# Two-bank PSUM reads for gelu, gate product, mask, exponential and remainder, with a new step list

## The chip, the cores and the metric

The kernel runs on one core of one Trainium2 chip. The time is the device time of one launch in microseconds. Three runs of the kernel before gave 258.43, 259.08 and 259.88 us; the median is 259.08 us.

## The reference, cut to what matters

A gated linear recurrence over 768 tokens feeds a GEGLU block with a gated residual.

```python
# attention: batch 4, heads 8, tokens 768, head size 48
scale = np.minimum(mag, 0.999) / (mag + 1e-06)        # mag = |a|
new_re = ar * S_re - ai * S_im                         # complex decay, per key row
new_im = ar * S_im + ai * S_re
S_re, S_im = (new_re + kv, new_im)                     # kv = k v^T
y[:, :, t] = np.einsum('bhd,bhde->bhe', q[:, :, t], S_re)
# feed-forward on x: [3072, 384], d_ff 1536
g, val = x @ w_gate, x @ w_val
ffn_out = (0.5 * g * (1 + erf(g / sqrt(2))) * val) @ w_out
out = x + ffn_out / (1 + exp(-(x @ w_res)))
```

## The kernel before, in words

The 768 tokens are cut into 6 chunks of 128. A *tile* is one batch and one chunk: 24 tiles of 128 tokens x 384 values. Tiles are grouped into 14 *units*; `SIZES` gives units of one tile (numbers 0, 1, 12, 13) and ten of two tiles. Each unit goes through three functions, which only record steps:

- `prepare`: loads a_re, a_im, q, k and v. ScalarE takes logarithms and exponentials (`ln`, `exp`, `lnb`), and arctangents. The decay's logarithm and its angle are each split into two 16-bit parts (`lh`, `ll`; `th`, `tl`) and summed over the tokens on TensorE with a triangular matrix (`cumL`, `cumT`, one PSUM bank for each tile). ScalarE evicts the first sums twice, as exp and exp of the negative (`pexpE`, `pexpI`, L427 and L428); from the second sums it takes the number of turns (`round`, L461), and VectorE the remainder of the angle (`fr`, L463). Sines, cosines and magnitudes make the features of q and k (`feat`), which are transposed on TensorE or by DMA.
- `attend`: per tile, eight heads of K^T Q in two banks of four heads (`qk`, L535); VectorE masks each bank (`am`, L538); `av` multiplies by v and adds the state's part; `kv` makes the state's update, which VectorE adds to the old state (`U`), and which is scaled by the decay into a bf16 copy (`Gb`) and an fp32 copy (`Gf`).
- `forward`: x is transposed; for each of six pairs of d_ff blocks, six matmuls fill a gate bank and six a value bank (`gv`, L606). ScalarE takes the gelu of the gate bank into an SBUF buffer (`gelu`, L611), VectorE multiplies it by the value bank (`h`, L612). `res` and `tanh` make the residual gate, `out` (L632) multiplies by w_out, `ot` and `otx` finish, and SP stores.

The steps are numbered as they are recorded: 1,442 of them. `ORDER` is a list of those numbers, written out by hand, and the instructions are issued in that order. Each engine so has a fixed sequence, and waits at its next instruction until what it needs is there. `PLACE` gives the engine for steps that VectorE, ScalarE or GpSimd could do. `Plan.run` also hands out buffers: at its first use each PSUM bank, tag `pb`, 8 of them, goes to the least recently ended one. Steps of VectorE and GpSimd that use a shared port (`TWO_PORTS`, and GpSimd's own work) are chained: where the list turns from one of the two engines to the other, the later step waits for the earlier. A new ScalarE function table is loaded where the list goes from one group of functions (log and exp; arctan and sine; gelu and tanh) to another: 33 times.

SP's queue issues the 120 loads, 28 transposes of features, 20 of x and 24 stores, also in list order; GpSimd's queue issues the weights and the small moves between chunks (`mrd`, `carry`).

Of the kernel before, what the change touches and what calls it, by code (L numbers as in the profile page):

```python
# [9 lines left out]
FP = mybir.dt.float32  # L10
# [8 lines left out]
SIZES = [(1, 1, 2)] + [(2, 2)] * 4 + [(2, 1, 1)]  # L19
PE_X = 3  # L20
PE_T = 6
WD = 21
WH = 8
TWO_PORTS = {"tai", "sq", "la", "lh", "ll", "abs", "th", "tl", "mrc", "qe", "feat", "vcast", "Gb", "Gf", "otx"}
# [5 lines left out]
    23: "POOL", 24: "POOL", 33: "DVE", 44: "POOL", 53: "ACT", 64: "ACT", 105: "DVE", 114: "ACT", 117: "POOL", 121: "DVE",  # L30
    145: "ACT", 190: "DVE", 191: "DVE", 203: "ACT", 213: "DVE", 223: "DVE", 227: "DVE", 228: "DVE", 230: "ACT", 252: "ACT",
    291: "DVE", 305: "DVE", 306: "DVE", 333: "POOL", 345: "ACT", 347: "ACT", 353: "DVE", 357: "DVE", 363: "DVE", 366: "POOL",
    408: "DVE", 422: "DVE", 423: "DVE", 438: "POOL", 446: "DVE", 456: "DVE", 460: "DVE", 469: "DVE", 472: "POOL", 482: "POOL",
    518: "DVE", 539: "DVE", 551: "ACT", 554: "ACT", 562: "DVE", 565: "POOL", 566: "POOL", 572: "DVE", 576: "DVE", 577: "DVE",
    579: "ACT", 588: "POOL", 595: "DVE", 598: "POOL", 670: "ACT", 671: "POOL", 681: "POOL", 682: "POOL", 689: "ACT",
    691: "ACT", 700: "POOL", 710: "POOL", 711: "DVE", 752: "DVE", 767: "POOL", 783: "POOL", 794: "POOL", 801: "ACT",
    803: "ACT", 812: "POOL", 822: "POOL", 823: "DVE", 858: "DVE", 894: "ACT", 902: "DVE", 905: "POOL", 913: "ACT", 924: "POOL",
    991: "POOL", 1003: "ACT", 1006: "POOL", 1017: "POOL", 1025: "ACT", 1042: "DVE", 1045: "POOL", 1080: "DVE", 1086: "DVE",
    1101: "POOL", 1113: "ACT", 1116: "POOL", 1117: "POOL", 1135: "ACT", 1137: "ACT", 1146: "POOL", 1190: "DVE", 1196: "DVE",
    1210: "DVE", 1224: "ACT", 1225: "POOL", 1235: "POOL", 1236: "POOL", 1255: "DVE", 1296: "DVE", 1325: "POOL", 1330: "DVE",  # L40
    1368: "DVE", 1388: "ACT", 1389: "POOL", 1393: "DVE", 1396: "POOL",
}
ORDER = [
# [66 lines left out]
class Store:  # L110


    def __init__(self, tag, bufs):
        self.tag, self.bufs, self.users, self.tile, self.index = tag, bufs, [], None, None
# [15 lines left out]
class Plan:  # L130
# [7 lines left out]
    def store(self, tag, bufs):  # L138
        return Store(tag, bufs)
# [50 lines left out]
def kernel(  # L190
# [13 lines left out]
    nc = tc.nc  # L204
# [476 lines left out]
```

## Time and profile before

The profiled execution took 259.86 us; its span, from the first to the last instruction, is 258.1 us, so 1.76 us lie around it. It is 0.78 us above the median.

| Engine | busy us | share of the span | instructions |
|---|---|---|---|
| TensorE (PE) | 219.4 | 85% | 2362 |
| VectorE (DVE) | 214.4 | 83% | 373 |
| ScalarE (ACT) | 210.4 | 82% | 358 |
| GpSimd (POOL) | 109.7 | 42% | 129 |

The granted clock of TensorE was full throughout. Busy time is the union of an engine's instructions. Two instructions that follow each other overlap by some tens of ns, so means times counts come out above it. A matmul's duration holds its pipeline, so a busy TensorE is not one that issues without a gap.

### The profile page before, as it was taken

What the parts mean: (1) busy time and instruction counts of PE and PEld (TensorE: products, weight loads), DVE (VectorE), ACT (ScalarE), POOL (GpSimd) and SP (SyncE); (2) the same over time, 40 slices, a digit from 0 to 9 for tenths busy, and PEclk for the clock granted to TensorE, in tenths of its full rate; (3) what the DMA queues carried; (4) which work ended last, traced back from release to release, by engine and by line L of the source; (5) the groups of instructions that cost most, each with busy time, mean ns of one, the idle gap of its engine ahead of it and who ended that gap; (6) DMA issues with size and microseconds to landing.
All of it is one profiled execution on the core that took longest, in us unless ns stands there. A gap on an engine that the chain in (4) does not pass through costs nothing.

```text
span 258.1 us, 6191 instructions
## 1 busy us (share of the span) xinstructions
PE 219.4 (85%) x2362; PEld 171.2 (66%) x2362; DVE 214.4 (83%) x373; ACT 210.4 (82%) x358; POOL 109.7 (42%) x129
## 2 busy tenths in 40 slices
PE   0132864769999999999789999999999999999993
PEld 0001453548877887787677767787887868887882
DVE  2499888997999999998988989889998967866363
ACT  5899869989999999999969989999999498331440
POOL 1424145437452395948816386716105514210011
PEclk9999999999999999999999999999999999999999
DMA  8999999997799999789998999799999967862221
GB/s 145 187 194 190 191 184 188 205 221 119 86 164 176 186 171 207 151 152 191 135 219 159 219 173 203 156 168 184 240 155 183 184 141 161 114 113 64 63 91 62
DMA packets 170621, 41.92 MB, mean 162 GB/s; under 512 B 164064, under 2 KB 170592, under 8 KB 170592
## 3 DMA queue, kind: packets, MB, share of 16 engines
q1 hardware_dynamic: 166144, 37.63, 84.0%
q0 software_dynamic: 4448, 3.90, 10.1%
q8 instruction: 18, 0.29, 0.5%
q14 instruction: 11, 0.09, 0.1%
HBM read 31.26 MB, written 4.72 MB: 139 GB/s over the span
## 4 chain that ended last, share of the span: by engine, by line
PE 59%; DVE 11%; DMA 9%; issue 7%; POOL 6%; SPq 4%; ACT 2%; DVEq 0%; POOLq 0%
PE pb L606 29%; PE pb L632 15%; PE pb L621 4%; SPq L383 4%; PE pb L369 3%; DVE h L612 3%; PE pb L535 3%; DMA q<-in_q_dram 2%; POOL t L407 2%; DMA mr<-E 2%; DMA KT<-fK 2%; DMA ai<-in_a_im_dram 2%; DMA t<-fr 2%; PE pb L547 1%; PE pb L504 1%
## 5 line engine op out<-in xcount | busy, mean ns | idle before, releaser
L611 ACT ACTIVATE h<-pb 128x512 bf16<-128x512 f32 (+1 forms) x84 | 41.3, 545 | 21.4 <-PE pb L606 21.0
L606 PE MATMUL pb<-xT,wg 128*128 128x256 bf16 (+1 forms) x504 | 57.0, 257 | 1.3 <-ACT sg L623 0.9
L606 PE MATMUL pb<-xT,wv 128*128 128x256 bf16 (+1 forms) x504 | 56.8, 257 | 0.6 <-DMA xT<-x 0.6
L612 DVE SCALAR_TENSOR_TENSOR h<-h,pb 128x512 bf16<-128x512 bf16 (+1 forms) x84 | 48.5, 603 | 10.4 <-ACT h L611 5.8
L632 PE MATMUL pb<-wo,h 128*128 128x384 bf16 x288 | 53.5, 326 | 0.0
L606 PEld LDWEIGHTS <-wg 128*128 128x128 bf16 x504 | 43.4, 98 | 8.0 <-issue 1.6
L606 PEld LDWEIGHTS <-wv 128*128 128x128 bf16 x504 | 43.3, 98 | 7.2 <-DMA xT<-x 0.8
L648 ACT ACT_TABLE_LOAD x33 | 42.3, 1283 | 1.3 <-PEq L665 0.7
L632 PEld LDWEIGHTS <-h 128*128 128x128 bf16 x288 | 26.5, 97 | 14.3 <-DVE h L612 0.2
L538 DVE TENSOR_TENSOR am<-pb,mask 128x512 bf16<-128x512 f32 x48 | 32.1, 681 | 3.4 <-PE pb L535 3.3
L639 POOL TENSOR_TENSOR ot<-ot,x 128x384 f32<-128x384 f32 x13 | 11.8, 913 | 46.7 <-DVE ot L636 21.7
L369 PEld LDWEIGHTS <-mask 128*128 128x128 bf16 x96 | 9.2, 106 | 27.4 <-issue 24.0
L535 PE MATMUL pb<-QT,KT 96*128 96x128 bf16 x192 | 18.5, 226 | 2.9 <-DMA KT<-fK 1.5
L636 DVE SCALAR_TENSOR_TENSOR ot<-sg,pb 128x384 f32<-128x384 f32 x24 | 13.0, 548 | 7.3 <-PE pb L632 3.3
L407 POOL TENSOR_TENSOR t<-t,ai 128x768 f32<-128x768 f32 (+1 forms) x9 | 13.8, 1542 | 11.0 <-DVE s L412 5.4
L535 PEld LDWEIGHTS <-KT 96*128 96x128 bf16 x192 | 14.1, 101 | 6.7 <-DMA KT<-fK 1.8
L369 PE MATMUL pb<-th,mask 128*128 128x384 f16 x24 | 9.0, 374 | 10.3 <-DVE th L344 10.3
L568 POOL TENSOR_TENSOR Gb<-U,M 96x384 bf16<-96x384 f32 x12 | 9.9, 823 | 15.6 <-DVE fQ L487 7.0
L621 PE MATMUL pb<-wr,xT 128*128 128x384 bf16 x72 | 15.6, 326 | 0.8 <-ACT xT L343 0.8
L573 POOL TENSOR_TENSOR Gf<-U,M 96x384 f32<-96x384 f32 x9 | 7.5, 828 | 19.4 <-DVE tl L455 7.1
L463 DVE SCALAR_TENSOR_TENSOR fr<-fr,pb 128x384 f32<-128x384 int32 x24 | 12.8, 545 | 2.2 <-ACT fr L461 2.2
L369 PE MATMUL pb<-lh,mask 128*128 128x384 f16 x24 | 9.1, 380 | 5.7 <-DVE lh L417 5.7
(89 smaller groups left out, 464.2 us busy)
## 6 DMA issues: line engine op xcount, KB each, us to landing
ar<-in_a_re_dram SPq DMA_DIRECT2D x24, 192.0 KB, 4.7
ai<-in_a_im_dram SPq DMA_DIRECT2D x24, 192.0 KB, 4.5
k<-in_k_dram SPq DMA_DIRECT2D x24, 192.0 KB, 4.3
q<-in_q_dram SPq DMA_DIRECT2D x24, 192.0 KB, 4.2
vf<-in_v_dram SPq DMA_DIRECT2D x24, 192.0 KB, 4.1
out_dram<-ot SPq DMA_DIRECT2D x24, 192.0 KB, 2.6
wg<-in_moe_w_gate_dram POOLq DMA_DIRECT2D x6, 192.0 KB, 6.0
wv<-in_moe_w_val_dram POOLq DMA_DIRECT2D x6, 192.0 KB, 4.3
```

Source lines behind the costliest of these rows:

```text
L369: nc.tensor.matmul(out=bank.tile, lhsT=mask[:, 0, :], rhs=x[:, i * DM:(i + 1) * DM], start=(j == 0), stop=(j == 1))
L407: add(e1, "tai", lambda: on[e1].tensor_tensor(out=F("t"), in0=F("t"), in1=flat(T("ai"), n), op=OP.mult), [s["ai"]], [s["t"]], n)
L463: add("DVE", "fr", lambda i=i: nc.vector.scalar_tensor_tensor(out=T("fr")[:, i], in0=T("fr")[:, i].bitcast(INT), scalar=-TWO_PI, in1=cth[i ...
L535: nc.tensor.matmul(out=ap.tile[:, h, :], lhsT=kT.tile[0:DD, u * H // 2 + h, :], rhs=qT.tile[0:DD, u * H // 2 + h, :], start=True, stop=True)
L538: add("DVE", "am", lambda u=u, am=am, ap=ap: nc.vector.tensor_tensor(out=am.tile[:, u * H // 2:(u + 1) * H // 2, :], in0=ap.tile, in1=mask ...
L606: nc.tensor.matmul(out=o_.tile[:, u, :], lhsT=w_[:, k_, (2 * m + u) * 128:(2 * m + u + 1) * 128], rhs=s["xT"].tile[:, k_, 0:n].rearrange(" ...
L611: add("ACT", "gelu", lambda gp=gp, hv=hv: nc.scalar.activation(out=hv(), in_=gp.tile, func=AF.Gelu), [gp], [hh], n, "G")
L612: add("DVE", "h", lambda vp=vp, hv=hv: nc.vector.scalar_tensor_tensor(out=hv(), in0=hv(), scalar=0.5, in1=vp.tile, op0=OP.mult, op1=OP.mul ...
L621: nc.tensor.matmul(out=rp.tile, lhsT=s["xT"].tile[:, k_, i, :], rhs=wr[:, k_, :], start=(k_ == 0), stop=(k_ == KF - 1))
L632: nc.tensor.matmul(out=op_.tile, lhsT=s["h2"].tile[:, k_, i * 128:(i + 1) * 128], rhs=wo[:, k_, :], start=(k_ == 0), stop=(k_ == NF - 1))
L636: add("DVE", "ot", lambda i=i, op_=op_, ot=ot: nc.vector.scalar_tensor_tensor(out=ot.tile, in0=sg[i].tile, scalar=1.0, in1=op_.tile, op0=O ...
L648: plan.run(ORDER, lambda table: nc.scalar.preload_act_table_set(ACT_SETS[table]), lambda ins, prev: tc.add_manual_dep(ins.ins, prev.ins.na ...
```

## The change: what it does, and the diff

PSUM becomes four fixed tiles of two banks. `Bank(width)` takes one bank or an aligned pair; a single bank is taken preferably beside one that is in use, so that pairs stay whole. What reads PSUM then covers two banks with one instruction:

- `gelu` and `h` of two-tile units: 128x1024 in place of 128x512, three of each for a unit in place of six. One-tile units put four d_ff blocks in one bank, so 128x512 in place of 128x256, again three in place of six. Their twelve matmuls are one step (`gw`).
- the mask of a tile: one 128x1024 instruction (`am2`) in place of two.
- `pexpE`, `pexpI`, `round` and `fr` of two-tile units: one 128x768 instruction in place of two of 128x384.

The gelu's results lie in six small buffers `hb` in place of two large `h2`. The state tiles of two batches share a buffer, and `U` and `Gf` work in place, so `Gf` now comes after `Gb`. A mask `tri` is made on GpSimd at the start and, with `WHOLE = 0`, used by nothing. The options `UG2` and `TN2` are off, so the state's update and tanh stay single. `ORDER` and `PLACE` are new; there are 1,270 steps and 32 table loads.

```diff
+GV2 = 1
+NB1 = 4
+AM2 = 1
+PX2 = 1
+RD2 = 1
 PLACE = { ... }   # new throughout
 ORDER = [ ... ]   # new throughout
...
-                x.index = min(range(x.bufs), key=lambda i: row[i])
-                assert row[x.index] < at[t]
-                row[x.index] = end
+                now = at[t]
+                if x.tag in wide and x.width == 1:
+                    x.index = min(range(x.bufs), key=lambda i: (row[i] >= now, row[i ^ 1] < now, row[i]))
+                else:
+                    x.index = min(range(0, x.bufs, x.width), key=lambda i: max(row[i:i + x.width]))
+                for i in range(x.index, x.index + x.width):
+                    assert row[i] < at[t]
+                    row[i] = end
...
+    banks = [psb.tile([128, 2, 512], FP, tag="ps%d" % i, name="ps%d" % i) for i in range(4)]
     class Bank(Val):
-        def __init__(self):
-            Val.__init__(self, plan.store("pb", 8))
+        def __init__(self, width=1):
+            Val.__init__(self, plan.store("pb", 8, width))
...
+        def tokens(kind, x, hi, lo):
+            if n == 2 and kind[1]:
+                pair = Bank(2)
+                bank = [(pair.part(), lambda i=i: pair.at(i, DM)) for i in range(n)]
...
+            if n == 2 and kind[1]:
+                return [([o for o, _ in bank], slice(0, 2), lambda: pair.both[:, :, 0:DM], 2)]
...
+            if AM2:
+                add("DVE", "am2", lambda am=am, pair=pair: nc.vector.tensor_tensor(
+                    out=am.tile, in0=pair.both.rearrange("p c (h t) -> p (c h) t", t=128),
+                    in1=mask.to_broadcast([128, H, 128]), op=OP.mult), aps, amh)
...
-                    src = Buf("U")
-                        out=src.tile[0:DD], in0=dk.tile[0:DD], in1=old.tile[0:DD], op=OP.add), [dk, old], [src])
+                add("DVE", "U", lambda dkv=dkv, v2=v2: nc.vector.tensor_tensor(out=v2(), in0=dkv(), in1=v2(), op=OP.add), dks, wr_, m)
...
+        nb = 4 // n if n > 1 else NB1
+        w2 = 2 if GV2 and n > 1 else 1
+        for m in range(NF // (nb * w2)):
+            for name, w_ in (("wg", wg), ("wv", wv)):
+                o_ = Bank(w2)
+                for y in range(w2):
...
+            add("ACT", "gelu", lambda gp=gp, hv=hv: nc.scalar.activation(out=hv(), in_=pv(gp), func=AF.Gelu), gs, [hh], sz, "G")
             add("DVE", "h", lambda vp=vp, hv=hv: nc.vector.scalar_tensor_tensor(
-                out=hv(), in0=hv(), scalar=0.5, in1=vp.tile, op0=OP.mult, op1=OP.mult), [vp], [hh], n)
+                out=hv(), in0=hv(), scalar=0.5, in1=pv(vp), op0=OP.mult, op1=OP.mult), vs, [hh], sz)
```

More of the change, by code (lines that the diff above doesn't have):

```diff
@@ L23 @@
 WH = 8
[L24 removed]
+TWO_PORTS = {"tai", "sq", "la", "cap", "lh", "ll", "abs", "th", "tl", "mrc", "qe", "feat", "vcast", "Gb", "Gf", "otx"}
 ISSUES = {"wgv", "wr", "wo", "mrd", "carry"}
@@ L29 @@
 PLACE = {
[L30 to L38, printed above, removed]
@@ L163, in run @@
         at, rows, given, table, last = {}, {}, set(), None, None
+        wide = {x.tag for t in self.steps for x in t.stores if x.width > 1}
         assert sorted(order) == list(range(len(self.steps)))
@@ L220 @@
     size = [len(u) for u in units]
+    groups, at = [], 0
+    for g in FWD:
+        groups.append(list(range(at, at + g)))
+        at += g
+    MT = max(sum(size[p] for p in g) for g in groups)
     ctx.enter_context(tc.manual_schedule())
@@ L229 @@
     mask = cst.tile([128, 1, 128], BF, name="mask")
+    tri = cst.tile([128, 128], FP, name="tri")
     one = cst.tile([128, 1], FP, name="one")
@@ L309, in tile, with part, at, both @@
             return self.store.tile
+    banks = [psb.tile([128, 2, 512], FP, tag="ps%d" % i, name="ps%d" % i) for i in range(4)]
     class Bank(Val):
-        def __init__(self):
-            Val.__init__(self, plan.store("pb", 8))
-        def make(self, shape, dt=FP):
-            self.store.tile = psb.tile(shape, dt, tag="pb%d" % self.store.index, name="pb")
-            return self.store.tile
+        def __init__(self, width=1):
+            Val.__init__(self, plan.store("pb", 8, width))
+        def part(self):
+            return Val(self.store)
+        def at(self, i, *shape, dt=FP):
+            j = self.store.index + i
+            x = banks[j // 2][:, j % 2]
+            if dt != FP:
+                x = x.bitcast(dt)
+            n = 1
+            for y in shape:
+                n *= y
+            x = x[:, 0:n]
+            return x if len(shape) == 1 else x.rearrange("p (a b) -> p a b", b=shape[1])
         @property
-        def tile(self):
-            return self.store.tile
+        def both(self):
+            return banks[self.store.index // 2]
     class Feat(Val):
@@ L362, with whole @@
     st = [dict() for _ in range(NU)]
-    Gf, Gb = [None] * B, [None] * B
+    Gf, Gb, Gs = [None] * B, [None] * B, {}
     def sums(bank, i, hi, lo):
-        bank.make([128, DM])
         for j, x in enumerate((hi, lo)):
-            nc.tensor.matmul(out=bank.tile, lhsT=mask[:, 0, :], rhs=x[:, i * DM:(i + 1) * DM], start=(j == 0), stop=(j == 1))
+            nc.tensor.matmul(out=bank, lhsT=mask[:, 0, :], rhs=x[:, i * DM:(i + 1) * DM], start=(j == 0), stop=(j == 1))
+    def whole(bank, i, x):
+        nc.tensor.matmul(out=bank, lhsT=tri, rhs=x[:, i * DM:(i + 1) * DM], start=True, stop=True)
     def flat(t, n):
@@ new lines, in tokens @@
+        def tokens(kind, x, hi, lo):
+            if n == 2 and kind[1]:
+                pair = Bank(2)
+                bank = [(pair.part(), lambda i=i: pair.at(i, DM)) for i in range(n)]
+            else:
+                bank = [(o, lambda o=o: o.at(0, DM)) for o in (Bank() for _ in range(n))]
+            for i in range(n):
+                if p < WHOLE:
+                    add("PE", "sum" + kind[0], lambda i=i: whole(bank[i][1](), i, F(x)), [s[x]], [bank[i][0]])
+                else:
+                    add("PE", "cum" + kind[0], lambda i=i: sums(bank[i][1](), i, F(hi), F(lo)), [s[hi], s[lo]], [bank[i][0]])
+            if n == 2 and kind[1]:
+                return [([o for o, _ in bank], slice(0, 2), lambda: pair.both[:, :, 0:DM], 2)]
+            return [([bank[i][0]], i, bank[i][1], 1) for i in range(n)]
@@ L429, in prepare @@
+        E, Ei = [], []
+        for src, i, view, m in tokens(("L", PX2), "la", "lh", "ll"):
+            E.append(s["E"].part())
+            Ei.append(s["Ei"].part())
+            act("pexpE", lambda i=i, view=view: nc.scalar.activation(out=T("E")[:, i], in_=view(), func=AF.Exp), src, [E[-1]], "L", m)
+            act("pexpI", lambda i=i, view=view: nc.scalar.activation(out=T("Ei")[:, i], in_=view(), func=AF.Exp, scale=-1.0), src, [Ei[-1]], "L", m)
         s["E"].writers = [x for v_ in E for x in v_.writers]
@@ L519, in f @@
             def f():
-                mp.make([DD, 2 * H])
-                nc.tensor.matmul(out=mp.tile[:, 0:n * H], lhsT=s["mr"].tile[0:n * H].rearrange("x u d -> x (u d)"),
+                nc.tensor.matmul(out=mp.at(0, n * H)[0:DD], lhsT=s["mr"].tile[0:n * H].rearrange("x u d -> x (u d)"),
                                  rhs=idf[0:n * H, 0:n * H], start=True, stop=True)
@@ L578, in forward, with f, state @@
-    def forward(p):
-        s, n = st[p], size[p]
-        s["xT"], s["h2"] = Buf("xT"), Buf("h2")
-        xT = [s["xT"].part() for _ in range(n)]
-        for i in range(n):
+            add(e5, "x", lambda i=i, yp=yp, e5=e5: copy(e5, s["x"].tile[:, i], yp.at(0, H, D)), [yp], [s["xi"][i]])
+        if units[p][0][1] == NC - 1:
+            return
+        c = units[p][0][1]
+        for js in ([list(range(n))] if UG2 else [[i] for i in range(n)]):
+            m, b = len(js), units[p][js[0]][0]
+            dk = Bank(m)
+            dks = [dk.part() for _ in js]
+            for y, i in enumerate(js):
+                def f(i=i, y=y, dk=dk):
+                    for h in range(H):
+                        nc.tensor.matmul(out=dk.at(y, H, D)[:, h, :], lhsT=s["K"].tile[:, i * H + h], rhs=s["v"].tile[:, i, h, :], start=True, stop=True)
+                add("PE", "kv", f, [s["K"], s["v"]], [dks[y]])
+            if m == 2:
+                cut = lambda t: t[0:DD]
+                dkv = lambda dk=dk: dk.both[0:DD, :, 0:DM].rearrange("p c (h d) -> p c h d", d=D)
+                mb = lambda: s["M"].tile[:, 0:2].rearrange("p c (h u) -> p c h u", u=1).to_broadcast([DD, 2, H, D])
+            else:
+                cut = lambda t, b=b: t[0:DD, b % 2]
+                dkv = lambda dk=dk: dk.at(0, H, D)[0:DD]
+                mb = lambda i=js[0]: s["M"].tile[:, i].rearrange("p (h u) -> p h u", u=1).to_broadcast([DD, H, D])
+            def state(tag):
+                key = (tag, b - b % 2, c)
+                if key not in Gs:
+                    Gs[key] = Buf("%s%d" % (tag, b - b % 2))
+                v_ = Gs[key].part()
+                return v_, (lambda cut=cut, g=Gs[key]: cut(g.tile))
+            nb, nbv = state("Gb")
+            olds = sorted({id(Gf[b + y]): Gf[b + y] for y in range(m)}.values(), key=id) if c else []
+            if c > 0:
+                fv = Gf[b].view
+                v2 = (lambda cut=cut, fv=fv: cut(fv()))
+                wr_ = olds
+                add("DVE", "U", lambda dkv=dkv, v2=v2: nc.vector.tensor_tensor(out=v2(), in0=dkv(), in1=v2(), op=OP.add), dks, wr_, m)
+                src, sv = wr_, v2
+            else:
+                src, sv = dks, dkv
+            e14 = place("DVE") if c else "DVE"
+            add(e14, "Gb" if c else "Gb0", lambda nbv=nbv, sv=sv, mb=mb, e14=e14: on[e14].tensor_tensor(
+                out=nbv(), in0=sv(), in1=mb(), op=OP.mult), src + [s["M"]], [nb], m)
+            for y in range(m):
+                Gb[b + y] = nb
+            if c < NC - 2:
+                if c == 0:
+                    nf, nfv = state("Gf")
+                    nf.view = lambda g=Gs["Gf", b - b % 2, c]: g.tile
+                    add("DVE", "Gf0", lambda nfv=nfv, sv=sv, mb=mb: nc.vector.tensor_tensor(
+                        out=nfv(), in0=sv(), in1=mb(), op=OP.mult), src + [s["M"]], [nf], m)
+                    for y in range(m):
+                        Gf[b + y] = nf
+                else:
+                    e6 = place("POOL")
+                    add(e6, "Gf", lambda sv=sv, mb=mb, e6=e6: on[e6].tensor_tensor(
+                        out=sv(), in0=sv(), in1=mb(), op=OP.mult), [s["M"]], src, m)
@@ L583, in forward @@
+    def forward(group):
+        tiles = [(p, i) for p in group for i in range(size[p])]
+        n = len(tiles)
+        xt = Buf("xT")
+        xT = [xt.part() for _ in tiles]
+        for j, (p, i) in enumerate(tiles):
+            s = st[p]
+            flat_x = lambda s=s, i=i: s["x"].tile[:, i].rearrange("p h d -> p (h d)")
             if p >= PE_X:
-                add("SP", "dX", lambda i=i: nc.sync.dma_start(
-                    out=s["xT"].tile[:, :, i, :], in_=s["x"].tile[:, i].rearrange("p h d -> p (h d)"), transpose=True), [s["xi"][i]], [xT[i]])
+                add("SP", "dX", lambda j=j, fx=flat_x: nc.sync.dma_start(out=xt.tile[:, :, j, :], in_=fx(), transpose=True), [s["xi"][i]], [xT[j]])
@@ L614, in forward @@
-        sg = [Buf("sg") for _ in range(n)]
-        for i in range(n):
-            rp = Bank()
-            def f(i=i, rp=rp):
-                rp.make([128, DM])
-                for k_ in range(KF):
-                    nc.tensor.matmul(out=rp.tile, lhsT=s["xT"].tile[:, k_, i, :], rhs=wr[:, k_, :], start=(k_ == 0), stop=(k_ == KF - 1))
-            add("PE", "res", f, [xT[i], W["wr", 0]], [rp])
-            add("ACT", "tanh", lambda i=i, rp=rp: nc.scalar.activation(out=sg[i].tile, in_=rp.tile, func=AF.Tanh, scale=0.5),
-                [rp], [sg[i]], 1, "G")
@@ new lines, in forward, with f @@
+        per = nb * w2
+        sg = []
+        step = 2 if TN2 and n > 1 else 1
+        for j in range(0, n, step):
+            rp, sgb = Bank(step), Buf("sg")
+            rps = [rp.part() for _ in range(step)]
+            for y in range(step):
+                def f(j=j + y, y=y, rp=rp):
+                    for k_ in range(KF):
+                        nc.tensor.matmul(out=rp.at(y, DM), lhsT=xt.tile[:, k_, j, :], rhs=wr[:, k_, :], start=(k_ == 0), stop=(k_ == KF - 1))
+                add("PE", "res", f, [xT[j + y], W["wr", 0]], [rps[y]])
+                sg.append((sgb, lambda y=y, sgb=sgb: sgb.tile[:, y * DM:(y + 1) * DM]))
+            add("ACT", "tanh", lambda rp=rp, sgb=sgb: nc.scalar.activation(
+                out=sgb.tile[:, 0:step * DM].rearrange("p (c m) -> p c m", m=DM),
+                in_=rp.both[:, :, 0:DM] if step == 2 else rp.at(0, 1, DM), func=AF.Tanh, scale=0.5), rps, [sgb], step, "G")
@@ L626, in forward, with f @@
+        for j, (p, i) in enumerate(tiles):
+            s, (b, c) = st[p], units[p][i]
             op_, ot = Bank(), Buf("ot")
             for lo in range(0, NF, 4):
-                def f(i=i, lo=lo, op_=op_):
-                    if lo == 0:
-                        op_.make([128, DM])
+                def f(j=j, lo=lo, op_=op_):
                     for k_ in range(lo, lo + 4):
-                        nc.tensor.matmul(out=op_.tile, lhsT=s["h2"].tile[:, k_, i * 128:(i + 1) * 128], rhs=wo[:, k_, :],
+                        u = k_ % per
+                        nc.tensor.matmul(out=op_.at(0, DM), lhsT=hb[k_ // per].tile[:, (u * n + j) * 128:(u * n + j + 1) * 128], rhs=wo[:, k_, :],
@@ L643 @@
     weights()
-    for p in range(NU):
-        prepare(p)
-        attend(p)
-        forward(p)
+    for g in groups:
+        for p in g:
+            prepare(p)
+            attend(p)
+        forward(g)
     plan.run(ORDER, lambda table: nc.scalar.preload_act_table_set(ACT_SETS[table]),
```

202 lines of the change are left out of this document (99 added, 103 removed), and 117 rows, old and new, of the table ORDER.

## The prediction

> **What bounds the kernel now.** I read the page first: engine totals and the 40 slices, then the stages, then groups by shape, then the order in time.
>
> ```profile
> PE 219.4 (85%) x2362; PEld 171.2 (66%) x2362; DVE 214.4 (83%) x373; ACT 210.4 (82%) x358; POOL 109.7 (42%) x129
> ...
> PE   0132864769999999999789999999999999999993
> ...
> DVE  2499888997999999998988989889998967866363
> ACT  5899869989999999999969989999999498331440
> ...
> DMA  8999999997799999789998999799999967862221
> ```
>
> Three engines are within 4% of each other, and TensorE's gaps lie in the first nine slices (to 58 us). The stages (busy us of PE, PEld, DVE, ACT, POOL, then clock, DMA share, GB/s):
>
> ```profile
> 0.00:60.00 60.00, 27.84 (x221) 18.13 (x222) 46.25 (x79) 51.15 (x84) 23.19 (x41) 1.00 1.15 189
> 60.00:88.00 28.00, 27.67 (x374) 23.40 (x371) 27.87 (x52) 26.81 (x46) 11.33 (x12) 1.00 0.94 141
> 88.00:130.00 42.00, 39.93 (x442) 31.79 (x440) 39.32 (x67) 40.66 (x66) 31.68 (x29) 1.00 1.02 170
> 130.00:200.00 70.00, 70.00 (x734) 54.45 (x732) 63.39 (x106) 66.08 (x112) 32.32 (x37) 1.00 1.06 186
> 200.00:254.00 54.00, 53.97 (x605) 43.42 (x602) 36.49 (x71) 25.71 (x52) 11.14 (x12) 1.00 0.57 112
> 254.00:258.10 4.10, 0.00 (x0) 0.00 (x0) 1.11 (x2) 0.00 (x0) 0.00 (x0) 1.00 0.25 96
> ```
>
> Busy TensorE includes pipeline time, so I price a matmul by the pace of a run of them. The chain of waits gives this (start, us, what):
>
> ```profile
> 136.34 2.60 PE pb L632 x16
> ...
> 199.92 3.93 PE pb L606 x36
> ```
>
> That is 0.163 us for 384 columns and 0.109 for 256. With 0.056 for 128 columns and 0.026 for the 48-column ones (timeline), the 2,362 matmuls need 205 us. Counted by shape, about 16.5 of them are issued by 60 us and 44 by 88 us. So from 60 to 254 us, 194 us, TensorE has some 188 us to issue: it is close to a full engine from 60 us on, and what is lost is mostly the start (43 us) and the end (4 us). But ScalarE and VectorE are at 94 to 99% in 60 to 130 us and 91 to 94% in 130 to 200 us: they set when TensorE is fed.
>
> **What the parts cost now.** Groups by shape (busy us, mean ns, then idle before):
>
> ```profile
> L611 ACT ACTIVATE h<-pb 128x512 bf16<-128x512 f32 x60 | 33.0, 610 | 11.0 <-PE pb L606 10.6
> L427 ACT ACTIVATE E<-pb 128x384 f32<-128x384 f32 x24 | 11.7, 491 | 0.6 <-POOL mr L344 0.5
> L405 ACT ACTIVATE t<-la 128x768 f32<-128x768 f32 x10 | 8.5, 856 | 0.1
> L611 ACT ACTIVATE h<-pb 128x256 bf16<-128x256 f32 x24 | 8.4, 383 | 10.4 <-PE pb L606 10.4
> ...
> L612 DVE SCALAR_TENSOR_TENSOR h<-h,pb 128x512 bf16<-128x512 bf16 x60 | 39.0, 680 | 5.8 <-PE pb L606 3.6 <-ACT h L611 2.0
> L538 DVE TENSOR_TENSOR am<-pb,mask 128x512 bf16<-128x512 f32 x48 | 32.1, 681 | 3.4 <-PE pb L535 3.3
> L463 DVE SCALAR_TENSOR_TENSOR fr<-fr,pb 128x384 f32<-128x384 int32 x24 | 12.8, 545 | 2.2 <-ACT fr L461 2.2
> L612 DVE SCALAR_TENSOR_TENSOR h<-h,pb 128x256 bf16<-128x256 bf16 x24 | 9.4, 413 | 4.6 <-ACT h L611 3.8 <-PE pb L606 0.8
> ```
>
> The means suggest a large fixed part, but neighbours overlap, as the timeline shows:
>
> ```profile
> 88.02 1.09 ACT L611 ACTIVATE h<-pb 128x512 bf16<-128x512 f32 x2
> ...
> 92.62 2.47 DVE L612 SCALAR_TENSOR_TENSOR h<-h,pb 128x512 bf16<-128x512 bf16 x4
> ```
>
> A gelu that follows another adds 1.09 - 0.61 = 0.48 us, not 0.61; a product adds (2.47 - 0.68)/3 = 0.60, not 0.68.
>
> **The change, part by part.**
>
> *Gelus.* From 256 to 512 columns a gelu grows by 227 ns, 0.887 ns a column. So 1024 columns last 0.61 + 0.45 = 1.06 us and add 0.93 in a run, against 2 x 0.475 = 0.95: 0.02 saved. For 42 merges (30 of two-tile units, 12 of one-tile units) that is 0.9 us of ScalarE.
>
> *Exponentials and turns.* From 384 to 768 columns such a form grows by some 0.34 us; a run's pace is 0.38 for one of 384, so 0.72 in place of 0.76. 30 merges at 0.04 to 0.05 give 1.3 us.
>
> A page states another price. The Trainium skill, "ScalarE: Activation LUTs", section "What ACT_TABLE_LOAD costs", says that back-to-back activations overlap by about 93 ns of a fixed 186, which would make each merge worth 93 ns; two of its 512-column gelus would take 1.13 us, and the trace shows 1.09. By it the 72 merges would give 6.7 us, and the sum below would be bounded by VectorE alone, at 254.3.
>
> *Products, masks, remainders.* From 256 to 512 columns h grows by 267 ns, so 512 more cost 0.534 us against 0.60 for a second instruction: 0.065 saved 30 times, 0.066 on each of the 12 narrow ones, 0.065 on 24 masks, 0.06 on 10 remainders, together 4.9 us of VectorE. Bounds, since no read over two banks is in the trace: if crossing costs as much as a second start, nothing; if the whole difference of a lone instruction counts (0.68 - 0.534), 0.146 each and 11 us. I take the pace, as these engines run without gaps in 60 to 200 us.
>
> *New engine choices.* Counting both lists, ScalarE loses 6 copies of x, 3 wide `abs`, 2 `cpX` and some small copies, gains 6 squares, and one table load goes (1.28 us): 3.4 us less. VectorE gains 6 copies of x, 3 wide `abs`, 2 `otx` and small ones, and loses 4 wide `tl` and 4 squares net: 1.5 more. GpSimd takes the 4 wide `tl` (1.64 each) and gives up squares and `otx`: 1.6 less. It is at 42%, but its chained port steps also hold VectorE; the turns between the two go from 66 to 64, so I put nothing on that. Its mask `tri` comes before its first input, which arrives after 5 us: hidden. SP issues the same 192 transfers, reordered; at about 1 us each in the first 60 us its queue stays as full as before.
>
> Sums by pace: ScalarE 201.3 to 195.7, VectorE 206.9 to 203.5, TensorE unchanged.
>
> *What is longer.* A merged product must wait for a gelu of 1.06 rather than 0.61 us, and a merged remainder for both tiles' sums: 0.7 us more in a unit's preparation (2.4 against 1.75). Neighbouring units' work covers it. `Gf` after `Gb` on GpSimd adds 0.82 us to a state that is needed a chunk later: also covered. If these covers fail, at 10 units, 7 us would be back.
>
> *New list.* As instructions go in list order, I added the pace of every step along both lists and noted how far an engine's handed-out work is ahead of TensorE's at a TensorE step. The span can't be below that lead, plus the engine's idle time up to there, plus TensorE's 205 us and the end.
>
> - Start: ScalarE's largest lead is 36.4 us before (at 42 us of TensorE's work; the trace has 44 issued at 88 us, with ScalarE idle for 10) and 33.0 after (at 30): 3.4 less. VectorE's largest is 29.7 and 24.9: 4.8 less.
> - Middle, at 144 us of TensorE's work: ScalarE 29.6 and 24.5, VectorE 21.5 and 19.2; at 120 us VectorE 25.0 and 23.1, 1.9 less.
>
> By 200 us, ScalarE has idled 15.3 us and VectorE 23.2 before, so lead plus idle is 44.9 and 44.7: both bind, beside TensorE's own 43 to 47. I take 3.4, the lead at the start, where TensorE's loss lies, with ends of 1.9 and 5.1 (29.6 - 24.5). The end stays 4 us: a product, a last `out`, `ot`, `otx` and a store in both.
>
> Sum: span 258.1 - 3.4 = 254.7, and 259.86 - 3.4 = 256.5 on the profiled execution's scale. That execution is 0.8 above the median, so I forecast **255.7**.
>
> **The rivals.**
>
> *Slower: TensorE waits for pairs.* A gate pair is held over twelve matmuls (1.31 us) and a gelu of 1.06; before, a bank over six (0.65) and 0.61. The place is the second `gv` pair of a unit. An extra wait is at most 1.064 - 0.610 = 0.45 us for each of 30 chunks, 13.6 us. From 8 chunks on it eats the 3.4; at 15 it gives 255.7 + 6.8 = 262.5. Against it: in the waits, ScalarE's gelus wait 21.0 us for TensorE, while TensorE hardly waits for a gelu. For it: four pairs are little where eight banks were.
>
> *Faster: VectorE leads the start.* The first unit's features come after 13.5 us of VectorE's list in place of 22.3, and the first gate matmuls at a lead of 20.4 in place of 27.9. If the start follows VectorE, 7.5 us go: 251.6. Against it, ScalarE's busy 51 of the first 60 us.
>
> *No change: loads set the start.* The DMA share is over 1 in 0 to 60 us, and the same 120 loads come in nearly the same order; then 259. Against it: ScalarE waits only 2.4 us for a_re and 4.1 for v in the whole span.
>
> *The change doesn't do what it says: banks of a pair wait for each other.* If a write to one bank waits for a read of its neighbour, the some 150 single banks lose up to 0.465 us each; a third of them gives 23 us, 279.
>
> **How the numbers follow.** Forecast 0.45 (own range 252.5 to 258); VectorE's start 0.18; no change 0.12; pairs 0.20; neighbours 0.05. Half a per cent, 1.3 us, is about what can be told from no change, so faster means below 257.8: 0.42 + 0.18 = 0.60; same 0.03 + 0.12 = 0.15; slower 0.25. The range 249.5 to 262.5 takes in the faster rival and the middle of the pair rival, and leaves out about 0.15 above and 0.05 below.
>
> **What would show it.** Right: gelus of 128x1024 at 1.0 to 1.1 us, products and masks of 1.2; ScalarE's busy time 203 to 206, VectorE's 209 to 212; first gate matmul some 3 us before 54 us; TensorE's busy time still near full from there. Wrong: TensorE waiting for gelus or for h in the waits, products above 1.3 us, or ScalarE and VectorE with more idle time in 60 to 200 us than 11 and 12 us (6.5 and 9.4 before).

## The result, and the profile after

The changed kernel takes 298.43 us (median; 296.93 to 298.64) against 259.48 for the kernel before on the same chip: 1.1465 times as long, 95% interval 1.141 to 1.1521. The forecast was 255.7 us, range 249.5 to 262.5. It is wrong in sign and in size.

The page of the changed kernel, engine totals and slices (the span is 296.9 us, so a slice is 7.4 us):

```profile
PE 234.2 (79%) x2362; PEld 178.5 (60%) x2362; DVE 212.4 (72%) x308; ACT 205.1 (69%) x275; POOL 108.4 (37%) x130
...
PE   0122674398589987999789899899699999989983
...
DVE  2549888818638889688687889898859787655262
ACT  3899989077675796979876977988776545642040
...
PEclk9999985579958999899959999999889999999999
DMA  8999999999412999549996998769867692752121
```

VectorE and ScalarE are busy for a little less time than before (212.4 and 205.1 us against 214.4 and 210.4). Yet every engine has holes, also TensorE, which was full from the tenth slice on. In slices 11 to 13 even the transfers nearly stop. The stages, in the prediction's cuts with one more at the end (busy us of PE, PEld, DVE, ACT, POOL, then clock, DMA share, GB/s):

```profile
0.00:60.00 60.00, 22.65 (x167) 15.44 (x168) 41.05 (x70) 44.85 (x62) 26.73 (x44) 0.86 1.28 191
60.00:88.00 28.00, 23.10 (x280) 18.32 (x278) 14.36 (x22) 21.48 (x29) 11.43 (x13) 0.80 0.67 114
88.00:130.00 42.00, 38.61 (x382) 29.62 (x380) 35.68 (x50) 32.73 (x41) 19.35 (x16) 0.93 0.82 144
130.00:200.00 70.00, 64.77 (x663) 49.58 (x661) 58.90 (x80) 57.26 (x77) 29.88 (x33) 0.95 0.84 148
200.00:254.00 54.00, 49.45 (x510) 38.45 (x508) 42.13 (x59) 34.52 (x47) 15.06 (x18) 0.97 0.77 142
254.00:297.00 43.00, 35.61 (x372) 27.07 (x369) 20.30 (x30) 14.25 (x22) 5.92 (x7) 0.98 0.32 73
```

No instruction of VectorE or ScalarE got slower by itself; only TensorE's granted clock fell, to 0.80 in 60 to 88 us. By 88 us TensorE has started 447 matmuls, where the kernel before had started 595, and it keeps falling behind in every stage to 254 us. From 60 to 200 us ScalarE is idle for 28.5 us and VectorE for 31.1; before it was 6.5 and 9.4. Three engines that all wait for each other point to dependences (who waits for whom), not to durations. The durations are those forecast (groups by shape: busy us, mean ns, idle before):

```profile
L709 DVE SCALAR_TENSOR_TENSOR hb<-hb,ps 128x1024 bf16<-128x1024 bf16 x30 | 36.0, 1215 | 2.1 <-PE ps L698 1.9
L708 ACT ACTIVATE hb<-ps 128x1024 bf16<-128x1024 f32 x30 | 30.0, 1023 | 16.0 <-PE ps L698 16.0
L597 DVE TENSOR_TENSOR am<-ps,mask 128x1024 bf16<-128x1024 f32 x24 | 29.2, 1219 | 16.7 <-PE ps L588 16.7
...
L515 DVE SCALAR_TENSOR_TENSOR fr<-fr,ps 128x768 f32<-128x768 int32 x10 | 9.5, 946 | 2.3 <-ACT fr L513 2.3
```

### The profile page after: what moved, and what is told of

It reads as the page before. It is cut to its first block, busy times and chain, and to the rows that moved or that the text cites. A ratio compares the mean times of both kernels' runs of the same rounds, so it can differ in the third digit from the quotient of the medians.

```text
span 296.9 us, 6080 instructions
## 1 busy us (share of the span) xinstructions
PE 234.2 (79%) x2362; PEld 178.5 (60%) x2362; DVE 212.4 (72%) x308; ACT 205.1 (69%) x275; POOL 108.4 (37%) x130
## 4 chain that ended last, share of the span: by engine, by line
PE 50%; DVE 13%; issue 11%; ACT 8%; POOL 6%; SPq 5%; DMA 5%; DVEq 0%; POOLq 0%; ACTq 0%
PE ps L698 21%; PE ps L733 15%; SPq L416 5%; PE ps L720 3%; DMA wg<-in_moe_w_gate_dram 3%; PE ps L555 3%; DVE hb L709 2%; PE ps L588 2%; PE ps L398 2%; POOL t L441 2%; DVE ot L737 2%; POOL tl L508 2%; DMA k<-in_k_dram 2%; DVE fr L515 1%; ACT CS L528 1%
## 5 line engine op out<-in xcount | busy, mean ns | idle before, releaser
L733 PE MATMUL ps<-wo,hb 128*128 128x384 bf16 x288 | 61.4, 356 | 7.2 <-DVE fr L515 2.6
L698 PE MATMUL ps<-xT,wg 128*128 128x256 bf16 (+1 forms) x504 | 58.2, 267 | 8.5 <-DMA wg<-in_moe_w_gate_dram 4.9
L708 ACT ACTIVATE hb<-ps 128x1024 bf16<-128x1024 f32 (+1 forms) x42 | 36.9, 901 | 30.1 <-PE ps L698 21.8
L698 PE MATMUL ps<-xT,wv 128*128 128x256 bf16 (+1 forms) x504 | 55.0, 257 | 0.4 <-DVE ot L737 0.3
L709 DVE SCALAR_TENSOR_TENSOR hb<-hb,ps 128x1024 bf16<-128x1024 bf16 (+1 forms) x42 | 44.0, 1062 | 3.9 <-PE ps L698 1.9
L733 PEld LDWEIGHTS <-hb 128*128 128x128 bf16 x288 | 29.2, 105 | 27.3 <-issue 15.2
L597 DVE TENSOR_TENSOR am<-ps,mask 128x1024 bf16<-128x1024 f32 x24 | 29.2, 1219 | 16.7 <-PE ps L588 16.7
L508 POOL TENSOR_TENSOR tl<-t,th 128x768 bf16<-128x768 f32 (+1 forms) x10 | 14.9, 1493 | 26.6 <-DVE th L374 8.3
L588 PE MATMUL ps<-QT,KT 96*128 96x128 bf16 x192 | 17.6, 229 | 1.5 <-DVE QT L374 0.8
L720 PE MATMUL ps<-wr,xT 128*128 128x384 bf16 x72 | 15.8, 334 | 1.8 <-DVE Gf L643 0.9
```

The lines of the kernel that those rows point to most:

```text
L508: add(e10, "tl", lambda: on[e10].tensor_tensor(out=F("tl"), in0=F("t"), in1=F("th"), op=OP.subtract), [s["t"], s["th"]], [s["tl"]], n)
L588: nc.tensor.matmul(out=view()[:, h, :], lhsT=kT.tile[0:DD, u * H // 2 + h, :], rhs=qT.tile[0:DD, u * H // 2 + h, :], start=True, stop=True)
L597: add("DVE", "am2", lambda am=am, pair=pair: nc.vector.tensor_tensor(out=am.tile, in0=pair.both.rearrange("p c (h t) -> p (c h) t", t=128) ...
L698: nc.tensor.matmul(out=o_.at(y, nb, n * 128)[:, u, :], lhsT=w_[:, k_, (nb * m + u) * 128:(nb * m + u + 1) * 128], rhs=xt.tile[:, k_, 0:n]. ...
L708: add("ACT", "gelu", lambda gp=gp, hv=hv: nc.scalar.activation(out=hv(), in_=pv(gp), func=AF.Gelu), gs, [hh], sz, "G")
L709: add("DVE", "h", lambda vp=vp, hv=hv: nc.vector.scalar_tensor_tensor(out=hv(), in0=hv(), scalar=0.5, in1=pv(vp), op0=OP.mult, op1=OP.mult ...
```

## Two suspects in the trace

**Late gate weights.** TensorE's order in time around 52 us (start, us, what, idle time before it):

```profile
51.72 0.95 PE L698 MATMUL ps<-xT,wg 128*128 128x128 bf16 x7
56.72 0.29 PE L698 MATMUL ps<-xT,wg 128*128 128x128 bf16 x1 [4.05 <-DMA wg<-in_moe_w_gate_dram]
57.82 0.61 PE L698 MATMUL ps<-xT,wg 128*128 128x128 bf16 x4 [0.81 <-DMA wg<-in_moe_w_gate_dram]
```

The gate weights come in two halves of 768 columns. A one-tile unit's step `gw` now fills four d_ff blocks, so its second instance reads columns 512 to 1023, which lie in both halves. The step names only one half as its input, and the new list puts that step among the first gate matmuls, while the second half's last two transfers are issued last of all gate and value weights. Seven matmuls run, and TensorE then stands before the eighth.

**Neighbours.** The matmul of `out` at 213 us:

```profile
212.47 0.55 DVE L515 SCALAR_TENSOR_TENSOR fr<-fr,ps 128x384 f32<-128x384 int32 x1 [0.68 <-ACT fr L513]
...
213.08 1.10 PE L733 MATMUL ps<-wo,hb 128*128 128x384 bf16 x4 [2.59 <-DVE fr L515]
```

This `out` writes the second bank of the fourth two-bank tile; `fr` reads the first bank of that tile. They share no data. A reader can wait for a stranger's matmuls in the same way, and pass the wait on:

```profile
145.37 0.55 DVE L643 TENSOR_TENSOR Gf<-ps,Gf 96x384 f32<-96x384 f32 x1 [2.22 <-PE ps L733]
...
146.72 1.21 DVE L597 TENSOR_TENSOR am<-ps,mask 128x1024 bf16<-128x1024 f32 x1
...
147.98 0.87 PE L698 MATMUL ps<-xT,wg 128*128 128x256 bf16 x6 [2.06 <-DVE am L597]
```

The state's update (L643, the step `U`) reads the second bank of the second tile and waits for an `out` that writes the first. The mask `am` stands behind it in VectorE's order and is late, and TensorE stops 2.06 us for the banks that `am` reads.

In the built program every instruction carries the semaphore values that it waits for, and so the instruction that it waits for can be looked up. In the changed program 96 waits are for an instruction that touches only the *other* bank of a two-bank tile: 58 of TensorE before a write, 38 of ScalarE and VectorE before a read. The program before has none. Set against the times of this trace, 45 of the 96 were the last thing that the instruction waited for, and cost 17.6 us on TensorE, 18.0 on VectorE and 8.5 on ScalarE, each counted from when all else was ready.

The theories were: *neighbours* (the two-bank tiles make strangers wait), *pair hold* (the prediction's slower rival: pairs are held longer and TensorE lacks banks), and *list* (order and late weights). The first two expectations below call the list A, pair hold and neighbours together B, and the late weights C.

## The experiments

**The list alone, and the weights alone.** The first kernel has the instructions of before, one bank each and each bank its own tile, in the new order and with the new engine choices (`U` and `Gf` in place and small gelu buffers, as in the changed kernel). The second is the changed kernel with the weight transfers in the order in which they are needed.

```diff
 # first: the kernel before
-ORDER, PLACE = (old)
+ORDER, PLACE = (new; a merged step as its halves, one after the other)
...
 # second: the changed kernel, ORDER only
-parts of all four halves mixed; two of the three parts of gate half 2 last
+gate half 1, gate half 2, w_res, value half 1, value half 2
```

> The new list and the new choice of engines with the old single-bank instructions: every merged step is split into its two halves at the same place of the list (gelu, h, am, exponentials, turns, remainders); gates and values of one-tile units are again six matmuls to a bank. The in-place state and small gelu buffers stay. Theory A (the list itself is the loss, the two-bank instructions are harmless): 290 to 300 us, with the same low clock. Theory B (a bank pair is held too long, or its halves wait for each other): 255 to 265. Theory C (the first gate block of a one-tile unit spans both weight halves, which the list did not reckon with; the late weights set everything off): here the split blocks need the halves one by one, so most of the loss goes: 262 to 275.

> The changed kernel with only the weight transfers in another order, in the same places of the list: gate halves one and two, the residual weights, value halves one and two. Theory C: the 5 us stall on the gate weights and the low clock at 45 to 62 us go, and with them most of the loss: 262 to 278. Theory A in the sense that the whole list fits badly: only that stall goes, 290 to 295. Theory B: 290 to 295.

Measured: 268.47 us (ratio 1.0322, 1.0277 to 1.0366) and 289.86 us (1.1125, 1.109 to 1.116). The list costs some 8 us without any merged instruction; the weights by need give back 8.6 of the 39, so the late weights are not the main cause (theory C expected 262 to 278 us from the second kernel). Some 30 us come with the merged instructions or their tiles.

**Tiles alone.** Three kernels with the old list, the old instructions and the same choice of banks. They differ only in how the eight banks are declared: eight tiles of one bank, four of two, one of eight.

```diff
+banks = [psb.tile([128, 512], FP, ...) for i in range(8)]      # first
+banks = [psb.tile([128, 2, 512], FP, ...) for i in range(4)]   # second
+banks = psb.tile([128, 8, 512], FP, ...)                       # third
...
-            self.store.tile = psb.tile(shape, dt, tag="pb%d" % self.store.index, name="pb")
+            x = banks[self.store.index]               # first
+            x = banks[self.store.index // 2][:, self.store.index % 2]   # second
+            x = banks[:, self.store.index]            # third
```

> The kernel before, its list, placement, instructions and choice of banks unchanged; only, a bank is no longer a new one-bank tile at each use but one of eight standing one-bank tiles. It is the control for the next kernel. Neighbour theory (banks that lie in one two-bank tile wait for each other's users): no two banks share a tile, so 258 to 262 us as before. Pair-hold theory (the wide instructions keep two banks until both are read, and TensorE lacks banks): no wide instruction here, 258 to 262. List theory (the new order is the cause): old order, 258 to 262. Above 265, standing tiles themselves cost time and the next kernel says nothing alone.

> As the control, but the eight banks are the halves of four standing two-bank tiles. Every instruction still reads or writes one bank, in the old order. Neighbour theory: TensorE now waits for the last user of the neighbour too. The trace of the changed kernel shows such waits of 2 to 4 us each behind fr, U and am; 5 to 12 of them give 270 to 290 us, with waits of the matmuls for steps whose own bank is another one. Pair-hold theory: no pair is taken, 258 to 262. List theory: 258 to 262.

> The control of the one-tile declaration: the kernel before, old list, single-bank instructions, its eight banks as one eight-bank tile. By the program's waits only a handful are for another bank, so 258 to 263 us like the eight one-bank tiles (261.1), not 343 like the four two-bank ones. If it is above 300, one tile is no cure and the two runs above say nothing.

Measured: 261.09 us (ratio 0.9989, 0.9954 to 1.0025), **343.13** (1.314, 1.3062 to 1.3218) and 260.85 (1.0007, 0.9972 to 1.0043). Not one wide instruction is in the second kernel, and it loses 82 us against the first. Of its waits in the built program some 250 are for the other bank of a tile; the first kernel has none, the third one. Two of them in the second kernel's order in time:

```profile
100.27 0.81 PE L615 MATMUL ps<-xT,wg 128*128 128x256 bf16 x6 [1.28 <-ACT sg L632]
...
105.91 0.27 PE L615 MATMUL ps<-xT,wg 128*128 128x256 bf16 x1 [0.69 <-ACT h L620]
```

Both times the gate bank is free; `sg` and `h` read the bank beside it. And readers wait for TensorE in turn, by the waits of the same kernel (us, times, longest) against those of the one-tile kernel:

```profile
ACT h L620 <- PE ps L615: 40.6, 26, 6.2
```

```profile
ACT h L620 <- PE ps L615: 21.4, 16, 4.8
```

That tiles of two banks make strangers wait, and how much it can cost, is shown. My guess of 270 to 290 was far too low.

**The same banks in the changed kernel, without neighbours.** First with the eight banks split, pairs in two two-bank tiles that are only taken whole, singles in four one-bank tiles (weights by need, list repaired by under one place in the mean):

```diff
+twos = [psb.tile([128, 2, 512], FP, ...) for i in range(2)]
+ones = [psb.tile([128, 1, 512], FP, ...) for i in range(4)]
...
-            Val.__init__(self, plan.store("pb", 8, width))
+            Val.__init__(self, plan.store("pp", 4, 2) if width == 2 else plan.store("pb", 4))
```

> The changed kernel with the weights by need (289.9 us), the same merged instructions and the same list but for small repairs (mean shift of a step under one place, at most 18), and with its eight banks split: pairs come from two two-bank tiles that are only ever taken whole, single banks from four one-bank tiles. Neighbour theory: nothing shares a tile but the halves of one pair, so the false waits go: 255 to 270 us, TensorE's busy time at 10 us in 10 from 70 us on. Pair-hold theory: the same pairs are held as long and there are fewer places for them, so 286 to 300. List theory: same order, 285 to 295.

Measured: 315.69 us (1.2042, 1.1959 to 1.2125), 26 us *slower* than the same kernel with shared tiles, though no wait for a neighbour is left; the neighbour theory had expected 255 to 270. Here TensorE waits for the users of its own pairs:

```profile
PE ps L713 <- ACT hb L723: 11.8, 13, 2.3
...
PE ps L713 <- DVE hb L724: 6.9, 7, 1.4
```

This speaks for pair hold, but it also took places away: a pair had four, now two, and the single banks have four of their own. The next two leave places, banks, list and instructions as they are in the changed kernel, and only declare the banks as one eight-bank tile, without and with the weights by need:

```diff
-    banks = [psb.tile([128, 2, 512], FP, tag="ps%d" % i, name="ps%d" % i) for i in range(4)]
+    banks = psb.tile([128, 8, 512], FP, tag="ps0", name="ps0")
...
-            x = banks[j // 2][:, j % 2]
+            x = banks[:, j]
...
-            return banks[self.store.index // 2]
+            return banks[:, self.store.index:self.store.index + 2]
```

> The changed kernel, every instruction, bank number, placement and list position as it is; only the eight banks are declared as one eight-bank tile in place of four two-bank tiles. In the program built so, no matmul or reader waits for a user of another bank (96 such waits in the changed kernel, none in the kernel before). Neighbour theory: the false waits go and the places stay, so what is left of the loss is the late gate weights (8.6 us by the run with the weights by need) and the list: 262 to 275 us. Pair-hold theory (TensorE lacks banks because a pair is held until its wide reader has ended; the four two-place run at 315.7 us speaks for it): pairs are held as long as before, 290 to 300.

> The run before this one and the weights by need together. Neighbour theory with late weights as second cause: 256 to 266 us, TensorE at 10 us of work in 10 from 65 us on, the granted clock above 0.97. If the two causes overlap (the weight stall had hidden other waits), less than 8.6 us comes back. Pair-hold theory: 280 to 292.

Measured: **264.55 us** (1.0136, 1.0072 to 1.0199) and **260.53 us** (1.0001, 0.9973 to 1.0029). One declaration is worth 33.9 us. Pair hold, which expected 290 to 300 and 280 to 292, falls for the changed kernel: in the waits of the two one-tile kernels TensorE waits for no gelu and no product, so with four places a pair is free in time. The stages of the second:

```profile
0.00:60.00 60.00, 27.81 (x268) 19.97 (x269) 44.20 (x73) 51.22 (x72) 26.72 (x45) 0.97 1.21 189
60.00:88.00 28.00, 25.05 (x314) 20.54 (x312) 24.72 (x40) 24.02 (x30) 13.19 (x15) 1.00 1.02 176
88.00:130.00 42.00, 41.44 (x469) 32.75 (x467) 40.39 (x56) 41.15 (x55) 28.27 (x24) 1.00 0.96 171
130.00:200.00 70.00, 68.83 (x728) 53.63 (x725) 64.07 (x86) 63.16 (x84) 28.30 (x33) 1.00 1.06 178
```

TensorE is full again from 88 us on, and the clock with it.

**The new list with single banks and the weights by need.** The first experiment's kernel with the second's order of weights.

> The new list and placement with the single-bank instructions of before (268.5 us), now with the weights by need. If the late weights are all that the new list costs, 258 to 262 us; if the order itself costs something, 263 to 268; if the singles did not suffer from the weights, 268.

Measured: 263.83 us (1.0127, 1.0068 to 1.0187): the order, with its engine choices, in-place state and small buffers, costs 3.4 us against the kernel before.

**Merged instructions in the old order.** A merged step stands where the later of its halves stood; first with two-bank tiles, then with one tile. (A first list of this kind, with fewer repairs, had no free bank at one step and so has no time.)

```diff
-ORDER, PLACE = (new)
+ORDER, PLACE = (old, merged; small repairs where no bank would be free)
```

> The changed kernel's merged instructions and two-bank tiles, with the steps in the order of the kernel before (a merged step where the later of its two halves stood, small repairs where a bank would not be free) and with its placement. Neighbour theory: single banks beside pairs still wait for the neighbour, 275 to 300 us. Pair-hold theory: 275 to 300 too. List theory: the old order brings it back, 256 to 264 us.

> The merged instructions in the old order (405.8 us), with the eight banks as one tile. If neighbour waits make the loss there too, most of the 145 us come back: 265 to 300. If it is the order, which is not made for steps that wait for both halves and take two banks at once, 330 to 390.

Measured: 405.80 us (1.5527, 1.5452 to 1.5602) and 366.59 (1.4027, 1.3954 to 1.41). Neighbours make 39 us here too, but 105 us stay with the order, which was not made for steps that wait for two halves and take an aligned pair. No theory had expected the first figure. Whether the place at the later half or the repairs do it was not tried.

**A list moved by estimate.** On the kernel of 260.53 us, 447 of 1,270 steps were moved (a step stands 3.6 places off in the mean over all), so that with the durations of the traces TensorE would wait less at the start.

> The run with one tile and the weights by need (260.5 us), with 447 of its 1,270 steps moved in the list by a few places (3.6 in the mean), so that with the durations of the traces TensorE waits less in the first 80 us. That run has issued 18.4 us of TensorE's work by 60 us and 35.4 by 80; TensorE's whole work is 214 us, so each microsecond more by 80 us is one off the end. If the merged instructions leave ScalarE and VectorE room that the list did not use: 253 to 258 us. If loads or the first units' chain of preparation set the start whatever the list: 259 to 262.

Measured: 271.51 us (1.038, 1.0322 to 1.0439), slower than either expected. TensorE's longest wait (us in all, times, longest), and then the stages:

```profile
PE ps L554 <- DVE fK L538: 13.9, 2, 11.1
```

```profile
0.00:60.00 60.00, 28.03 (x256) 20.93 (x257) 42.41 (x71) 49.88 (x69) 25.74 (x44) 0.89 1.23 191
60.00:88.00 28.00, 22.94 (x301) 18.60 (x300) 22.80 (x38) 22.83 (x29) 15.08 (x14) 1.00 0.88 155
...
130.00:200.00 70.00, 66.55 (x689) 51.51 (x688) 63.03 (x83) 62.60 (x84) 30.85 (x35) 1.00 0.88 167
```

TensorE stands 11.1 us for the features of k, but it is not there that the time goes. Counted by shape at the prediction's paces, it has issued 16.8 us of work by 60 us, against 17.3 in the kernel whose list was moved; by 80 us it is 30.7 against 33.2, by 200 us 142.4 against 148.8, and by 250 us 188.2 against 198.1. The loss is spread over the run after 60 us, and which moved steps make it was not separated. None of these kernels beats the kernel before; the best one equals it.

## Why the prediction was wrong, point by point

The runs give a sum, from the kernel before (260.40 us beside the one-tile runs) to the changed one (timed beside 259.48 us of before):

| step | from, to (us) | worth |
|---|---|---|
| new list and engine choices, weights in time | 260.40, 263.83 | +3.4 |
| merged instructions | 263.83, 260.53 | -3.3 |
| late gate weights | 260.53, 264.55 | +4.0 |
| two-bank tiles | 264.55, 298.43 | +33.9 |

The late weights cost 4.0 us alone and 8.6 beside the two-bank tiles (298.43 to 289.86), so the last two lines depend on their order. The first line also holds the in-place state and the small buffers.

- **Durations: right.** The gelu of 1024 columns was put at 1.06 us and takes 1.02, the products and masks at 1.21 and take 1.215 and 1.219, the exponentials at 0.83 (0.49 + 0.34) and take 0.805. ScalarE's busy time was put at 203 to 206 and is 205.1; VectorE's at 209 to 212 and is 212.4, just above.
- **What a merge saves: near in sum, shared out otherwise.** From the single-bank kernel to the merged one, same list, ScalarE's busy time falls from 208.1 to 203.8 us and VectorE's from 216.3 to 211.8: 4.3 and 4.5, where 2.2 and 4.9 were forecast. For ScalarE's 72 merges that is 60 ns each, between my 31 from the rows and the 93 of the Trainium skill's "ScalarE: Activation LUTs", section "What ACT_TABLE_LOAD costs"; the measurement decides.
- **The step that failed: the sum puts nothing on waits between the banks of one two-bank tile.** The runs show +33.9 us there, by the declaration alone. The last rival, "banks of a pair wait for each other", had the mechanism, but it got 0.05 and lay outside the range, and the prediction names no row against it. The traces of before could not speak on it, because there each bank was a tile of its own, so that there were no such waits to see; the built program of the changed kernel holds them. The rival's size was off too: I counted only writes that wait for a read, at 0.465 us each, and came to 279. In the changed kernel readers wait for strangers' matmuls as well (26.5 of the 44 us), and a wait is as long as whatever the neighbour is behind in, 2.59 us in the line above and not one eviction.
- **"New engine choices", the queues: a step left out.** It said that SP's transfers are the same, and nothing of the weights on GpSimd's queue. That `gw` reads across both halves stands in the diff (`NB1 = 4`); the weights' place in the new list was not held against it. 4.0 us.
- **The lead at the start, -3.4: did not come; in the mended kernel it came and was lost.** Counted by shape at the prediction's paces, from the matmuls started in the traces (203.2 us in all), the kernel with both faults mended has issued 17.3 us of TensorE's work by 60 us against 15.1 before: the lead is there; the changed kernel itself has 10.8. (The prediction counted 16.5 for before, and the expectation of the moved list 18.4 of 214 for the mended kernel; both are rougher counts.) By 70 us it is 25.9 against 24.0, by 75 us 28.9 against 29.1, by 130 us 81.4 against 80.8. The lead was given back between 70 and 75 us, at two waits that no lead of a list shows:

```profile
70.11 2.11 PE L732 MATMUL ps<-wo,hb 128*128 128x384 bf16 x12 [0.85 <-DMA wo<-in_moe_w_out_dram]
74.14 0.40 PE L587 MATMUL ps<-QT,KT 96*128 96x128 bf16 x4 [1.93 <-DVE KT L373]
```

  So the sum's -3.4, read from the leads along the two lists, is in no run: the list with its engine choices took +3.4, the merges gave -3.3, and together they are the kernel before. That -3.3 is so close to -3.4 is chance.
- **"Slower: TensorE waits for pairs" (0.20): fell** for four places, by the one-tile runs. With two places it may well be what makes 315.69.
- **The signs of being wrong: one of three came.** ScalarE's and VectorE's idle time in 60 to 200 us rose to 28.5 and 31.1 us. TensorE's waits for gelus and products, the sign of the pair rival, are 0.9 us in all, and no product takes 1.3 us. The first gate matmul does start 2 to 3 us before 54 us, as forecast, and stalls after seven.

## What to carry to other kernels

When a change joins buffers in one tile, ask at which grain waits are set for that tile, and look into the built program for waits between instructions that share no data: 96 of them cost 33.9 us here, and declaring the same banks as one tile removed them. A merged instruction saves tens of ns; price first what its halves and its neighbours now wait for, and hold every merged step against the place of each of its inputs in the list, weights too. Where TensorE is full already, as here from 60 us on, work saved on other engines counts only where TensorE still waits.

## What was not expected of the hardware

The clock can fall after shorter stops than I would have thought. In the changed kernel, stretches around the wait of 2.06 us for `am` shown above (clock is the third number from the end):

```profile
140.00:146.00 6.00, 5.92 (x66) 4.21 (x62) 3.62 (x6) 5.77 (x8) 3.63 (x5) 1.00 0.92 132
146.00:148.00 2.00, 0.02 (x1) 0.11 (x2) 1.93 (x2) 1.17 (x2) 1.06 (x1) 1.00 1.34 186
149.00:155.00 6.00, 5.13 (x30) 2.82 (x27) 5.37 (x8) 4.67 (x6) 1.35 (x1) 0.50 0.95 165
156.00:162.00 6.00, 6.00 (x66) 5.00 (x64) 4.24 (x7) 4.21 (x5) 1.31 (x2) 1.00 0.44 86
```

After two idle microseconds TensorE ran at half clock for all of the six us shown, and started 30 matmuls where 66 stand in the stretches before and after; the mean clock over the run is 0.923. The Trainium skill's "TensorE: Matmul & The Clock Gate", section "Why this matters for your kernels", asks for no idle gap above some 3 us; here the clock fell after 2.06 us. That is no bound either: in the kernel with the moved list a longer stop was followed by full clock.

```profile
65.95 1.07 PE L554 MATMUL ps<-ident,fK 128*128 128x128 bf16 x16 [2.81 <-DVE fK L538]
```

```profile
66.00:72.00 6.00, 4.86 (x89) 4.63 (x90) 4.90 (x8) 3.10 (x5) 4.38 (x4) 1.00 1.17 177
```

What decides between the two stays open. How much of the 33.9 us is clock can be bounded: by mean clock and span of the profiled executions, (1 - 0.923) x 296.9 = 22.9 us of full clock were withheld in the changed kernel and (1 - 0.964) x 262.9 = 9.5 us with one tile and late weights. So, as an estimate, at most some 13 of the 33.9 us are clock, and at least some 20 are waiting.

Second, the same banks are watched bank by bank in a tile of eight and as a whole in a tile of two. This is no matter of the chip but of how waits are set when the program is built, and its reason stays open.
